# Retention attention with four experts on one Trainium2 core: k^T v as whole-array products early in each tile, a regrouped start of tile 1, and mixing-weight transposes ahead of the first expert product

## The chip, the cores and the metric

The kernel runs on one core of a Trainium2 chip. The metric is device microseconds (us) of one execution. The kernel before took 561.68 us, the median of four runs (560.77, 561.09, 562.26 and 562.52 us). The profiled execution is the one of 560.77 us; the span of its recorded work is 558.9 us.

## The reference, cut to what matters

First comes a causal attention with a decay per head and no softmax, for 8 batches of 8 heads, 576 positions and 64 channels; then four experts whose outputs are mixed by weights that come with each token.

```python
scores = scale * np.matmul(q, k.transpose(0, 1, 3, 2))
Dmat = np.where(rel >= 0, gamma[:, None, None] ** rel[None, :, :], 0.0)
ret = np.matmul(scores * Dmat, v)             # (8, 8, 576, 64)
x = ret.transpose(0, 2, 1, 3).reshape(4608, 512)
p = domain_probs / (domain_probs.sum(-1, keepdims=True) + 1e-09)
for e in range(4):
    h = np.maximum(x @ w1[e], 0.0)            # 512 -> 1024
    out += p[:, e:e + 1] * (h @ w2[e])        # 1024 -> 512
```

## The kernel before, in words

**Experts.** The 4608 tokens are cut into nine tiles of 512. `moe(nt)` is a generator that issues one tile, and each `yield` ends a group. Of each expert it issues eight groups "up" (`up`, L514: four 128x512 matmuls that accumulate over the 512 channels into a PSUM tile `ph`, then ScalarE's Relu into `hT`, L533) and four groups "down" (L543: eight 128x512 matmuls into `po`, then the weighted sum into `acc`: on ScalarE for expert 0, L547, on VectorE for the others, L549). So a tile has 48 groups: groups 0 to 7 are up and 8 to 11 down of expert 0, 12 to 19 up of expert 1, 24 to 31 up of expert 2, 36 to 43 up and 44 to 47 down of expert 3. `ph` and `po` share three PSUM banks (`ps_mm`).

With `lead=3`, as tiles 0 and 1 have it, the first three up groups are split by columns: first the left 256 tokens of all three, then, group by group, the right 256. The extra yields let other work stand in between.

**Attention.** A tile needs `xT`, the attention's output transposed. Tile nt reads tokens of batches nt-1 and nt (a batch is 576 tokens), so the attention of later batches is issued between the expert groups. `plan` holds, for each tile, what is called after which group; the order on every engine is the order of issue. Four chunks of 128 positions and a remainder of 64 make a batch. GpSimd casts k, q and v to bf16 (`km`, `qm`, `vm`, remainder `krb`, `qrb`, `vrb`; L235 to L243); k carries its decay. The transposes `qkT` come from TensorE in batches 0 and 1 (`T`, `Tc`, `Trem`) and from SyncE's transposing DMAs in batches 2 to 7 (`dmaT`, L268, issued by `begin` after the casts; then follow the loads of the next batch, on the same queue). Scores: `S`, `Sc`, `Srem`, masked on VectorE into `sT`. Outputs: products of masked scores with v (`O_values`, L351, and L358 for the remainder), then products of q with the running sum of k^T v over earlier chunks (`O_states`, L365, and L371), and a VectorE product with the decay `gq` into `xT`.

**k^T v.** The running sum stands in `sbd`, one 128x128 block for each chunk and pair of heads, of which the two diagonal 64x64 blocks are used. In batches 2 to 7 `kv_all` (L389) runs once per batch after group 24: 32 matmuls with 64 columns of k as weights and 64 columns of v moving, one per chunk and head, even heads into PSUM partitions 0 to 63 and odd heads into 64 to 127. `kv_sum` then adds the four chunks up: ScalarE copies the first, VectorE makes three sums (L406, L408), GpSimd puts them into `sbd` (L403). In batch 1 `kv(c)` (L250) does the same per chunk, accumulating in PSUM (`kvp`, one bank), with two ScalarE copies per chunk (L255). Batch 0 has its own class, `AttP`.

**Batch 1 and the start of tile 1.** `Tc(c)` follows groups 40, 42, 44 and 46 of tile 0; after the next group come `Sc(c)`, `Oc(c-1)` and `kv(c)`. `Sc(3)` comes after group 47. Then two steps of tile 1 are taken by hand (the left halves of its three first up groups), and then `Oc(3)`, whose `xT` the right halves need.

**Start.** Batch 0's loads and casts, the first expert's weights (`load_w1(0, ...)`, L125, `load_w2(0)`, L130, issued by GpSimd), then `late_constants` and the other experts' weights, on GpSimd too. `mixing_weights` transposes the mixing probabilities on TensorE (L206) after group 1 of tile 0 and normalises them on VectorE. The remainder's loads of batch 0 wait until `w2` of expert 0 has landed.

Of the kernel before, what the change touches and what calls it, by code (L numbers as in the profile page):

```python
# [20 lines left out]
def kernel(  # L21
# [84 lines left out]
    def load_rem(b, gate=None):  # L106
        for n, src in SRC:
            if n == "v":
                t = state[b]["vr"] = raw.tile([128, NP, D], FP32, tag="vr", name="raw_vr")
                for j in range(2):  # L110
                    nc.sync.dma_start(out=t[64 * j:64 * j + 64],
                                      in_=src[b, j:H:2, SM:S, :].rearrange("h p d -> p h d"))
                continue
            state[b][n + "r"] = raw.tile([R, H, D], FP32, tag=n + "r", name=f"raw_{n}r")
            i = nc.sync.dma_start(out=state[b][n + "r"], in_=src[b, :, SM:S, :].rearrange("h p d -> p h d"))
            if gate is not None and n == "k":
                after(i, gate)
# [38 lines left out]
    make_identity(nc, ident)  # L156

# [6 lines left out]
    identf = const.tile([NTT, NTT], FP32)  # L164


    trir = const.tile([128, R], BF16)

    def late_constants():
        nc.gpsimd.memset(tri, 1.0)  # L170
        nc.gpsimd.memset(trir, 1.0)
        for j in (0, 64):
            nc.gpsimd.affine_select(out=trir[j:j + 64], in_=trir[j:j + 64], compare_op=mybir.AluOpType.is_ge,
                                    fill=0.0, base=0, channel_multiplier=-1, pattern=[[1, R]])
        nc.gpsimd.affine_select(out=tri, in_=tri, compare_op=mybir.AluOpType.is_ge, fill=0.0,
                                base=0, channel_multiplier=-1, pattern=[[1, 128]])
        nc.gpsimd.tensor_copy(identf, ident[:NTT, :NTT])
# [25 lines left out]
    def mixing_weights():  # L203
        pp = ps_at.tile([128, E, NTT], FP32, tag="at", name="pp")
        for e in range(E):
            nc.tensor.transpose(pp[:, e, :], probs_raw[:, :, e], identf)  # L206
        nc.vector.tensor_copy(probs, pp)
        nc.vector.tensor_reduce(psm, probs[:, :, :].rearrange("p e t -> p t e"),
                                axis=mybir.AxisListType.X, op=ADD)
        nc.vector.tensor_scalar_add(psm, psm, 1e-9)  # L210
        nc.vector.reciprocal(psm, psm)
        nc.vector.tensor_tensor(probs, probs, psm[:, :].unsqueeze(1).to_broadcast([128, E, NTT]), op=MULT)
# [7 lines left out]
    class Att:  # L220
        rem_states = (NCH - 1,)

        def __init__(self, b):
# [3 lines left out]
            self.r = {n: att1.tile([R, H, D], BF16, tag=n + "r", name=n + "rb") for n in "kq"}  # L227
            self.r["v"] = att1.tile([128, NP, D], BF16, tag="vr", name="vrb")
# [16 lines left out]
        def kv(self, n):  # L245
            if n == 0:
                self.kvp = ps_kv.tile([128, NP, D], FP32, tag="kv", name="kvp")
            for p in range(NP):
                for j in range(2):
                    nc.tensor.matmul(  # L250
                        self.kvp[64 * j:64 * j + 64, p, :], lhsT=self.m["k"][:, n, 2 * p + j, :],
                        rhs=self.m["v"][:, n, 2 * p + j, :],
                        start=(n == 0 and p == 0), stop=(n == NCH - 1), skip_group_check=True)
            for j in (0, 64):
                nc.scalar.activation(sbd[j:j + 64, n, :, j:j + 64], self.kvp[j:j + 64], Copy)  # L255
# [75 lines left out]
        def Srem(self):  # L331
            s = ps_at.tile([128, NP, R], FP32, tag="at", name="sr")
            for p in range(NP):
                for j in (0, 64):
                    r = slice(j, j + 64)
                    nc.tensor.matmul(s[r, p, :], lhsT=self.qkT[r, 1, p, SM:S], rhs=self.qkT[r, 0, p, SM:S],
                                     start=True, stop=True, skip_group_check=True)
            self.srem = s

        def Srem_mask(self):  # L340
            st = self.sT["r"] = att1.tile([128, NP, R], BF16, tag="sTr", name="sTr")
            nc.vector.tensor_tensor(st, self.srem, trir[:, :].unsqueeze(1).to_broadcast([128, NP, R]), op=MULT)


        def O_values(self, pairs, rem=False):
            self.os = [ps_at.tile([128, SM], FP32, tag="at", name="o") for _ in pairs]
            self.orem = ps_at.tile([128, NP, R], FP32, tag="at", name="orem") if rem else None
            for p, o in zip(pairs, self.os):
# [5 lines left out]
            if rem:  # L354
                for p in range(NP):
                    for j in (0, 64):
                        r = slice(j, j + 64)
                        nc.tensor.matmul(self.orem[r, p, :], lhsT=self.r["v"][r, p, :], rhs=self.sT["r"][r, p, :],  # L358
                                         start=(p == 0), stop=False, skip_group_check=True)

        def O_states(self, pairs, rem=False):
            b = self.b
            for p, o in zip(pairs, self.os):
# [4 lines left out]
            if rem:  # L368
                for n in self.rem_states:
                    for p in range(NP):  # L370
                        nc.tensor.matmul(self.orem[:, p, :], lhsT=sbd[:, n, p, :], rhs=self.qkT[:, 0, p, SM:S],  # L371
                                         start=False, stop=(p == NP - 1), skip_group_check=True)
            for p, o in zip(pairs, self.os):
                nc.vector.tensor_tensor(xT[:, p, b * S:b * S + SM], o, gq[:, p, 0:SM], op=MULT)  # L374
            if rem:
                nc.vector.tensor_tensor(xT[:, :, b * S + SM:(b + 1) * S], self.orem, gq[:, :, SM:S], op=MULT)

        def Orem(self):
            self.O_values([], rem=True)
            self.O_states([], rem=True)  # L380


        def kv_all(self):
            self.kvp = [ps_kv.tile([128, 2, NP, D], FP32, tag="kv", name="kva"),
                        ps_at.tile([128, 2, NP, D], FP32, tag="at", name="kvb")]
            for n in range(NCH):
                for p in range(NP):
                    for j in range(2):
                        nc.tensor.matmul(self.kvp[n // 2][64 * j:64 * j + 64, n % 2, p, :],  # L389
                                         lhsT=self.m["k"][:, n, 2 * p + j, :], rhs=self.m["v"][:, n, 2 * p + j, :],  # L390
                                         start=(n % 2 == 0 and p == 0), stop=True, skip_group_check=True)

        def kv_sum(self):
            ksum = att1.tile([128, NCH, NP, D], FP32, tag="ksum", name="ksum")
            parts = [self.kvp[n // 2][:, n % 2] for n in range(NCH)]

            def put(eng, src, n):
                for j in (0, 64):
                    r = slice(j, j + 64)
                    if eng is nc.scalar:  # L400
                        eng.activation(sbd[r, n, :, r], src[r], Copy)  # L401
                    else:
                        eng.tensor_copy(sbd[r, n, :, r], src[r])  # L403

            put(nc.scalar, parts[0], 0)
            nc.vector.tensor_copy(ksum[:, 0], parts[0])  # L406
            for n in range(1, NCH):
                nc.vector.tensor_tensor(ksum[:, n], ksum[:, n - 1], parts[n], op=ADD)  # L408
                put(nc.gpsimd, ksum[:, n], n)
# [99 lines left out]
    def moe(nt, lead=0):  # L509
# [8 lines left out]
        for e in range(E):  # L518
            hT = hpool.tile([128, NFC, NT], BF16, tag="hT")
            for fc in range(NFC):  # L520
                if e == 0 and fc < lead:
                    if fc == 0:
                        early = [ps_mm.tile([128, NT], FP32, tag="mm", name="ph") for _ in range(lead)]
                        for x in range(lead):
                            up(early[x], e, x, slice(0, NT // 2))
                            if x != 1:
                                yield
                    ph = early[fc]
                    up(ph, e, fc, slice(NT // 2, NT))
# [29 lines left out]
    tiles = [moe(nt, lead=3 if nt < 2 else 0) for nt in range(n_nt)]  # L559
# [4 lines left out]
    for x, (hf, u) in enumerate(UNITS):  # L564
# [16 lines left out]
        a0.kv(hf, u)  # L581
    next(tile0)
# [13 lines left out]
    for nt in range(n_nt):  # L596
# [5 lines left out]
        if nt == 0:  # L602
# [3 lines left out]
            at(22, a0.Srem, a0.Srem_mask)  # L606
# [13 lines left out]
            for c, g in enumerate((40, 42, 44, 46)):  # L620
                at(g, lambda c=c: state["a1"].Tc(c))
                if c < 3:
                    at(g + 1, lambda c=c: state["a1"].Sc(c))
                if c > 0:
                    at(g + 1, lambda c=c: state["a1"].Oc(c - 1))
                at(g + 1, lambda c=c: state["a1"].kv(c))
        elif nt + 1 < B:
            if nt == 1:
# [3 lines left out]
                at(4, a1.Srem, a1.Srem_mask)  # L632
                at(6, a1.Orem)
            def begin(b=nt + 1):
# [10 lines left out]
            at(7 if nt == 1 else 0, begin)  # L645
            at(19 if nt == 1 else 17, lambda: state["A"].S([0, 1]))
            at(24, lambda: state["A"].Srem(), lambda: state["A"].O_values([0, 1]),
               lambda: state["A"].kv_all(), lambda: state["A"].kv_sum(), lambda: state["A"].Srem_mask())
            at(28, lambda: state["A"].O_states([0, 1]))
            at(30, lambda: state["A"].S([2, 3]))  # L650
            at(34, lambda: state["A"].O_values([2, 3], rem=True), lambda: state["A"].O_states([2, 3], rem=True))
# [3 lines left out]
        if nt == 0:  # L655
            state["a1"].Sc(3)
            next(tiles[1])
            next(tiles[1])
            state["a1"].Oc(3)
# [30 lines left out]
```

## Time and profile before

| | |
|---|---|
| median of four runs | 561.68 us |
| profiled execution | 560.77 us |
| its span | 558.9 us |
| granted TensorE clock, mean | 1.0 |
| up and down products, 128x512, back to back | 6.91 us for 32 |
| one steady tile (from one tile's first expert-0 down group to the next's: 153.26 to 212.96 us, 212.96 to 272.65 us) | 59.7 us |
| ScalarE Relu of an up group | 597 ns |
| ScalarE copy of one chunk's k^T v half, 64x256 | 378 ns |
| VectorE sum of a down group | 751 ns |

TensorE's matmuls are recorded with a modelled end, so they overlap in the records; the distance from one start to the next start is what a matmul takes of the stream. A line of the timeline gives a group's start, the time it covers, engine, line, operation, tiles and count, and in brackets what the engine waited for. A few records are missing, so that a group can count 15 matmuls where 16 ran.

### The profile page before, as it was taken

The page shows a single profiled execution, that of the slowest core. Times are in us where ns is not written, and L with a number is a line of the kernel's source. Part 1 is how long each engine was busy: PE and PEld are TensorE (multiplying, and loading weights), DVE is VectorE, ACT ScalarE, POOL GpSimd, SP SyncE. Part 2 cuts the span into 40 slices and gives each one's busy share as a digit, 9 for nine tenths or more (in the row PEclk, how much of TensorE's full clock was granted, in tenths as well). Part 3 has the DMA queues.
Part 4 walks back from the last instruction along what each step waited for, and adds up shares of the span by engine and source line. Part 5 has one row for each costly group of instructions (what it writes and reads, how often), then busy time and mean ns, then how long its engine had stood idle before and what let it go on. Part 6 is the DMA issues. An engine that isn't in the chain of part 4 may idle for free.

```text
span 558.9 us, 8453 instructions
## 1 busy us (share of the span) xinstructions
PE 546.2 (98%) x3469; PEld 262.8 (47%) x3530; DVE 165.7 (30%) x283; ACT 216.9 (39%) x371; POOL 109.5 (20%) x182
## 2 busy tenths in 40 slices
PE   8899999999999999999999999999999999999997
PEld 4544454454445444454445444544444444444443
DVE  5402261253214520462035212542046202220222
ACT  6452344433353235223433334323532353335332
POOL 7611257026002520044002600260010000000000
PEclk9999999999999999999999999999999999999999
DMA  8999999491369025910594058703300100010001
GB/s 233 180 202 200 206 204 234 102 210 20 106 132 178 1 86 96 215 21 38 114 182 83 0 123 149 143 1 96 65 2 1 74 2 0 1 75 1 1 0 75
DMA packets 148277, 53.83 MB, mean 96 GB/s; under 512 B 130668, under 2 KB 142188, under 8 KB 148240
## 3 DMA queue, kind: packets, MB, share of 16 engines
q1 hardware_dynamic: 141296, 44.79, 39.0%
q0 software_dynamic: 6800, 8.39, 8.8%
q8 instruction: 27, 0.44, 0.4%
q10 hardware_dynamic: 144, 0.13, 0.1%
q14 instruction: 10, 0.08, 0.1%
HBM read 45.16 MB, written 9.44 MB: 98 GB/s over the span
## 4 chain that ended last, share of the span: by engine, by line
PE 90%; DMA 5%; SPq 3%; POOL 1%; issue 1%; DVE 0%; POOLq 0%
PE po L543 43%; PE ph L514 41%; DMA wt<-in_moe_w_dram 2%; SPq L268 1%; PE o L351 1%; PE s L276 1%; DMA raw_v<-in_v_dram 1%; DMA raw_k<-in_k_dram 1%; PE o L365 1%; SPq L85 1%; SPq L91 1%; DMA qkT<-km 0%; POOL km L423 0%; PE ptc L297 0%; PE orem L358 0%
## 5 line engine op out<-in xcount | busy, mean ns | idle before, releaser
L533 ACT ACTIVATE hT<-ph 128x512 bf16<-128x512 f32 x288 | 171.6, 597 | 275.1 <-PE ph L514 275.1
L514 PE MATMUL ph<-xT,wt 128*128 128x512 bf16 (+1 forms) x1149 | 258.3, 375 | 2.4 <-DVE xT L329 0.8
L543 PE MATMUL po<-wt,hT 128*128 128x512 bf16 (+1 forms) x1126 | 254.0, 378 | 3.1 <-DMA wt<-in_moe_w_dram 1.3
L543 PEld LDWEIGHTS <-hT 128*128 128x128 bf16 x1160 | 112.6, 98 | 134.1 <-DMA wt<-in_moe_w_dram 1.8
L514 PEld LDWEIGHTS <-wt 128*128 128x128 bf16 x1176 | 112.7, 98 | 129.1 <-issue 0.9
L549 DVE SCALAR_TENSOR_TENSOR acc<-po,probs,acc 128x512 f32<-128x512 f32 (+1 forms) x109 | 81.3, 746 | 234.2 <-PE po L543 226.3
L283 DVE TENSOR_TENSOR sT<-s,tri 128x512 bf16<-128x512 f32 x48 | 29.8, 684 | 113.4 <-PE s L276 113.4
L403 POOL CAST sbd<-ksum 64x256 bf16<-64x256 f32 x36 | 14.3, 396 | 221.8 <-DVE ksum L408 197.7
L547 ACT ACTIVATE acc<-po,probs 128x512 f32<-128x512 f32 x36 | 24.7, 687 | 39.7 <-PE po L543 38.7
L235 POOL TENSOR_TENSOR km<-raw_k,gk 128x512 bf16<-128x512 f32 x28 | 29.2, 1042 | 14.2 <-DMA raw_k<-in_k_dram 10.2
L237 POOL CAST vm<-raw_v 128x512 bf16<-128x512 f32 x28 | 17.2, 614 | 42.3 <-PE o L351 35.0
L237 POOL CAST qm<-raw_q 128x512 bf16<-128x512 f32 x28 | 17.1, 609 | 7.6 <-DMA raw_q<-in_q_dram 7.1
L374 DVE TENSOR_TENSOR xT<-o,gq 128x512 bf16<-128x512 f32 x24 | 15.5, 686 | 7.6 <-PE o L365 7.6
L240 POOL TENSOR_TENSOR krb<-raw_kr,gk 64x512 bf16<-64x512 f32 x8 | 8.3, 1036 | 13.1 <-DMA raw_kr<-in_k_dram 12.8
L276 PEld LDWEIGHTS <-qkT 64*128 64x128 bf16 x192 | 5.4, 94 | 5.5 <-issue 4.7
L276 PE MATMUL s<-qkT 64*128 64x128 bf16 x192 | 7.6, 217 | 0.2 <-DMA qkT<-km 0.2
L351 PE MATMUL o<-sT,vm 128*64 128x128 bf16 x192 | 7.6, 222 | 0.0
L351 PEld LDWEIGHTS <-vm 128*64 128x64 bf16 x192 | 5.7, 109 | 2.8 <-issue 2.5
L140 PE MATMUL warm_out<-warm_in 128*128 128x512 bf16 x14 | 5.2, 524 | 1.3 <-DVE warm_in L135 1.3
L406 DVE COPY ksum<-kva 128x256 f32<-128x256 f32 x6 | 2.5, 425 | 11.8 <-ACT sbd L401 11.8
L365 PE MATMUL o<-qkT,sbd 128*128 128x128 bf16 x72 | 6.0, 220 | 0.0
L313 DVE TENSOR_TENSOR sT<-s,tri 128x512 bf16<-128x512 f32 x8 | 5.1, 684 | 2.0 <-PE s L309 2.0
(94 smaller groups left out, 146.3 us busy)
## 6 DMA issues: line engine op xcount, KB each, us to landing
out_dram<-acc SPq DMA_DIRECT2D x35, 256.0 KB, 2.0
raw_k<-in_k_dram SPq DMA_DIRECT2D x32, 256.0 KB, 5.0
raw_q<-in_q_dram SPq DMA_DIRECT2D x32, 256.0 KB, 5.2
raw_v<-in_v_dram SPq DMA_DIRECT2D x32, 256.0 KB, 5.1
wt<-in_moe_w_dram POOLq DMA_DIRECT2D x7, 1024.0 KB, 24.8
wt<-in_moe_w_dram POOLq DMA_DIRECT2D x2, 512.0 KB, 5.6
raw_kr<-in_k_dram SPq DMA_DIRECT2D x8, 128.0 KB, 5.4
raw_qr<-in_q_dram SPq DMA_DIRECT2D x8, 128.0 KB, 5.0
```

Source lines behind the costliest of these rows:

```text
L235: eng.tensor_tensor(o, i, gk[:, c, :].unsqueeze(2).to_broadcast([128, H, D]), op=MULT)
L237: eng.tensor_copy(o, i)
L276: nc.tensor.matmul(s[j][:, c, :], lhsT=self.qkT[r, 1, p, cs], rhs=self.qkT[r, 0, p, cs], start=True, stop=True)
L283: nc.vector.tensor_tensor(st[:, j], s[j], tri[:, :].unsqueeze(1).to_broadcast([128, NCH, C]), op=MULT)
L351: nc.tensor.matmul(o[64 * j:64 * j + 64, c * C:(c + 1) * C], lhsT=self.m["v"][:, c, 2 * p + j, :], rhs=self.sT[p][:, j, c, :], start=(c == ...
L374: nc.vector.tensor_tensor(xT[:, p, b * S:b * S + SM], o, gq[:, p, 0:SM], op=MULT)
L403: eng.tensor_copy(sbd[r, n, :, r], src[r])
L514: nc.tensor.matmul(ph[:, ts], lhsT=w1_sb[e][:, dc, fc * 128:(fc + 1) * 128], rhs=xT[:, dc, n0 + ts.start:n0 + ts.stop], start=(dc == 0), s ...
L533: nc.scalar.activation(hT[:, fc, :], ph, Relu)
L543: nc.tensor.matmul(po, lhsT=hT[:, fc, ns * 128:(ns + 1) * 128], rhs=w2_sb[e][:, fc, d:d + w], start=(fc == 0), stop=(fc == NFC - 1))
L547: nc.scalar.activation(a, po, Copy, scale=pe)
L549: nc.vector.scalar_tensor_tensor(a, po, pe, a, op0=MULT, op1=ADD)
```

## The change

- `kv(n, pairs)` is now one matmul per chunk and pair of heads, 128 columns of k as weights and 128 of v moving; only the diagonal blocks of the result are copied. It accumulates over the chunks in one PSUM bank, and two ScalarE copies per chunk put the running sum into `sbd`. `kv_all` and `kv_sum` are gone.
- In batches 2 to 7 the four `kv` follow groups 9, 11, 13 and 15 of a tile (13, 15, 17 and 18 of tile 1). `O_values` and `O_states` are one function again, `O`, issued after groups 24 and 32; the second `S` follows group 27, not 30.
- The remainder's v has the layout of k and q: one load instead of two (`load_rem`); `Srem` writes two PSUM tiles and is masked by two VectorE products with a corner of `tri`; `trir` is gone.
- Batch 1: `Tc` follows groups 39, 41, 43 and 45, and `kv(c)`, `Sc(c)`, `Oc(c-1)` follow the group after; `Oc(3)` follows group 47. Nothing of tile 1 is issued ahead of it.
- Tile 1 splits its first two up groups at column 384 (left 384 of both, then right 128 of each), not its first three at column 256.
- The transposes of the mixing probabilities are issued before the first up group of tile 0 and use a bank of `ps_mm`; `identf`, which they need, is made at the kernel's start instead of in `late_constants`.

```diff
-            for p in range(NP):
-                for j in range(2):
-                    nc.tensor.matmul(
-                        self.kvp[64 * j:64 * j + 64, p, :], lhsT=self.m["k"][:, n, 2 * p + j, :],
-                        rhs=self.m["v"][:, n, 2 * p + j, :],
-                        start=(n == 0 and p == 0), stop=(n == NCH - 1), skip_group_check=True)
+            for i, p in enumerate(pairs):
+                h = slice(2 * p, 2 * p + 2)
+                nc.tensor.matmul(
+                    self.kvp[:, p, :], lhsT=flat(self.m["k"][:, n, h, :]), rhs=flat(self.m["v"][:, n, h, :]),
+                    start=(n == 0 and i == 0), stop=(n == NCH - 1), skip_group_check=True)
+            a, z = pairs[0], pairs[-1] + 1
             for j in (0, 64):
-                nc.scalar.activation(sbd[j:j + 64, n, :, j:j + 64], self.kvp[j:j + 64], Copy)
+                nc.scalar.activation(sbd[j:j + 64, n, a:z, j:j + 64],
+                                     self.kvp[j:j + 64, a:z, j:j + 64], Copy)
...
-    tiles = [moe(nt, lead=3 if nt < 2 else 0) for nt in range(n_nt)]
+    tiles = [moe(0, lead=3, pause=True), moe(1, lead=2, cut=3 * NT // 4)] + [moe(nt) for nt in range(2, n_nt)]
...
         a0.kv(hf, u)
+    transposed_probs()
     next(tile0)
...
-            for c, g in enumerate((40, 42, 44, 46)):
+            for c, g in enumerate((39, 41, 43, 45)):
                 at(g, lambda c=c: state["a1"].Tc(c))
-                if c < 3:
-                    at(g + 1, lambda c=c: state["a1"].Sc(c))
+                at(g + 1, lambda c=c: state["a1"].kv(c, allp), lambda c=c: state["a1"].Sc(c))
                 if c > 0:
                     at(g + 1, lambda c=c: state["a1"].Oc(c - 1))
-                at(g + 1, lambda c=c: state["a1"].kv(c))
+            at(47, lambda: state["a1"].Oc(3))
...
+            for n, g in zip(range(NCH), (13, 15, 17, 18) if nt == 1 else (9, 11, 13, 15)):
+                at(g, lambda n=n: state["A"].kv(n, allp))
             at(19 if nt == 1 else 17, lambda: state["A"].S([0, 1]))
-            at(24, lambda: state["A"].Srem(), lambda: state["A"].O_values([0, 1]),
-               lambda: state["A"].kv_all(), lambda: state["A"].kv_sum(), lambda: state["A"].Srem_mask())
-            at(28, lambda: state["A"].O_states([0, 1]))
-            at(30, lambda: state["A"].S([2, 3]))
-            at(34, lambda: state["A"].O_values([2, 3], rem=True), lambda: state["A"].O_states([2, 3], rem=True))
+            at(24, lambda: state["A"].Srem(), lambda: state["A"].O([0, 1]))
+            at(27, lambda: state["A"].S([2, 3]))
+            at(32, lambda: state["A"].O([2, 3], rem=True))
...
-            state["a1"].Sc(3)
-            next(tiles[1])
-            next(tiles[1])
-            state["a1"].Oc(3)
```

## The prediction

> **What bounds the kernel.** I read the page's shares and the chain that ended last, then the list of waits, then TensorE's timeline at the places that the change touches.
>
> ```profile
> PE 546.2 (98%) x3469; PEld 262.8 (47%) x3530; DVE 165.7 (30%) x283; ACT 216.9 (39%) x371; POOL 109.5 (20%) x182
> ...
> PE 90%; DMA 5%; SPq 3%; POOL 1%; issue 1%; DVE 0%; POOLq 0%
> ```
>
> TensorE is 98% busy and makes 90% of the chain; no other engine is above 39%. So a change counts by what it adds to TensorE's stream or takes out of it, or by a wait there. The list of waits has three on the way:
>
> ```profile
> PE po L543 <- DMA wt<-in_moe_w_dram: 1.3, 1, 1.3
> ...
> PE ph L514 <- DVE xT L329: 0.8, 1, 0.8
> ...
> PE s L276 <- DMA qkT<-km: 0.2, 1, 0.2
> ```
>
> The first is the first down group waiting for expert 0's `w2`, at 27.4 us; the second the right halves of tile 1's first up groups waiting for batch 1's last `xT`; the third batch 2's scores waiting for its last transposing DMA. Together 2.3 us: more than that no rearrangement of waits can bring.
>
> Then TensorE's stream around group 24 of tile 1, which is the same in tiles 2 to 6:
>
> ```profile
> 114.78 1.03 PE L514 MATMUL ph<-xT,wt 128*128 128x512 bf16 x4
> 115.74 0.31 PE L336 MATMUL sr<-qkT 64*64 64x64 bf16 x8
> 115.98 0.64 PE L351 MATMUL o<-sT,vm 128*64 128x128 bf16 x16
> 116.45 0.42 PE L389 MATMUL kva<-vm,km 128*64 128x64 bf16 x16
> 116.70 0.42 PE L389 MATMUL kvb<-vm,km 128*64 128x64 bf16 x16
> 117.06 3.63 PE L514 MATMUL ph<-xT,wt 128*128 128x512 bf16 x15
> 120.52 0.50 PE L365 MATMUL o<-qkT,sbd 128*128 128x128 bf16 x6
> 120.86 1.89 PE L514 MATMUL ph<-xT,wt 128*128 128x512 bf16 x8
> ```
>
> Only starts matter. A 128x512 matmul takes 6.91/32 = 0.216 us, an up group 0.864, a down group 1.73. The four at 114.78 end at 115.64, but the next, on quarter arrays, start at 115.74: going from whole array to parts costs 0.10 us. The 32 `kv_all` matmuls run from 116.45 to 117.06; 0.10 of that is the way back to the whole array (the 16 `s` from 122.68 to 123.23, 0.55 us, carry the same), so they take 0.51, 16 ns each: the two column halves run side by side. The six `o` at L365, whole array and 128 columns, take 120.86 - 120.52 = 0.34, 56 ns each, and no pause before or after: 117.06 + 16 x 0.216 = 120.52.
>
> **The change, part by part.**
>
> *k^T v in batches 2 to 7.* Removed: 0.51 us per batch. Added: 16 whole-array matmuls of 128 columns, which the trace has at L365: 16 x 56 ns = 0.90, in four places without a change of array form. `O` keeps its three changes of form. So +0.39 us per batch, +2.34 for six: all on the path, since TensorE is the bound. The eight transposes of a `Tc`, whole array and 128 columns too, give 0.45/8 = 56 again. What these rows do not show is a pause ahead of the first of four, which waits for GpSimd and ScalarE: at least 0, at most the 0.10 of a change of form, 24 x 0.10 = 2.4 in all. I take 0, since the first `o` at L365 also waits for another engine's `sbd` and follows without a pause. The Trainium skill, "TensorE: Matmul & The Clock Gate", section "Back-to-back issue gap", speaks harder against the change: it gives about 81 ns per 128-column matmul in a stream of weight loads and matmuls. An estimate from that figure is 6 x (16 x 0.081 - 0.51) = 4.7 us for the six batches instead of 2.3. L365 is such a stream at 56, so the row decides.
>
> What goes with `kv_sum`, three VectorE sums and six GpSimd casts per batch, was off the path (VectorE 30%, GpSimd 20%): nothing gained. GpSimd's casts for the next batch may start after group 15 instead of 24; SyncE's transposes and loads stay behind the tile's output stores, so no transfer moves in tiles 2 to 6. ScalarE gets 8 copies instead of 2 per batch, 6 x 378 ns = 2.3 us in a tile of 59.7 with ScalarE 39% busy; in up groups it idles 0.27 us of each 0.864. It matters through one wait: the chunks accumulate in one PSUM bank, so `kv(n+1)` waits until ScalarE has copied `kv(n)`, and those copies queue behind a Relu. The rows:
>
> ```profile
> 116.91 0.77 ACT L401 ACTIVATE sbd<-kva 64x256 bf16<-64x256 f32 x2 [0.41 <-PE kva L389]
> 118.13 0.60 ACT L533 ACTIVATE hT<-ph 128x512 bf16<-128x512 f32 x1 [0.45 <-PE ph L514]
> 118.99 0.60 ACT L533 ACTIVATE hT<-ph 128x512 bf16<-128x512 f32 x1 [0.27 <-PE ph L514]
> ```
>
> A pair of copies is 0.77, a Relu 0.60, and it starts 0.2 after its group. Stepped through tile 1 from the end of group 13 (0.224 for `kv` and 0.864 per group, so groups 14 to 18 end at 1.09, 1.95, 3.04, 3.90 and 4.99): copies of chunk 0 until 1.45 us, of chunk 1 until 3.40, Relus of 16 and 17 until 4.69, copies of chunk 2 from 4.58 (engine times overlap by 0.1) to 5.35. But chunk 3 is due after group 18, at 4.99. TensorE stands 0.43 us, and group 19 and the scores stand behind it. In tiles 2 to 6 the last two are two groups apart (13, 15): copies end at 3.40 after group 11, TensorE wants 3.90; 0.5 spare, no wait. Also no `ph` bank is late: Relus stay within two groups.
>
> *Batch 1 and tile 1's start.*
>
> ```profile
> 82.84 0.40 PE L309 MATMUL s<-qkT 64*128 64x128 bf16 x8
> 83.17 1.48 PE L514 MATMUL ph<-xT,wt 128*128 128x256 bf16 x12
> 84.58 0.44 PE L322 MATMUL oc<-sT,vm 128*64 128x128 bf16 x8
> 84.95 0.40 PE L327 MATMUL oc<-qkT,sbd 128*128 128x128 bf16 x4
> 86.13 1.47 PE L514 MATMUL ph<-xT,wt 128*128 128x256 bf16 x12 [0.78 <-DVE xT L329]
> 87.53 0.29 PE L261 MATMUL ptr<-ident,qrb 64*128 64x64 bf16 x4
> ```
>
> I rebuilt the stretch from the first `Tc` (67.60 us, now 66.73, a group sooner) to `Trem` at 87.53. Blocks, as the starts of before give them: four `Tc` at 0.447; four `kv` at 0.224; four `Sc` at 0.095 + 0.327; the `Oc` 0.346, 0.57, 0.57 and, alone, 0.665; four up 3.454 and four down 6.908; tile 1's two split groups 8 x 0.162 + 8 x 0.056 (384 and 128 columns at the rate of 512) and a whole one, 2.61; 0.095 to `Trem`. Sum 19.59, so `Trem` starts at 86.32: 1.21 us sooner. Of that 0.78 is the wait, the rest changes of form (`kv` had to go back to column halves after the whole-array part of `Oc`). The wait goes because the left 384 columns (1.30 us) now stand behind `Oc(3)` and cover the 0.96 us that `xT` needed (84.95 + 0.22 to 86.13); VectorE's sum of group 47 (0.75) comes first, which leaves 0.2 us to spare. If that cover fails, up to 0.78 returns. Casts are in time: `vm` of chunk 1 ends at 69.6 us, its `kv` now at 70.9; `qm` of chunk 2 at 71.75, its `Tc` at 72.7.
>
> *What is late next.* Batch 2's scores after group 19 of tile 1. TensorE reaches them at 106.92 before; now -1.21 + 0.90 (four `kv`) + 0.43 (the stall) = 107.04. Their last transposing DMA lands at 107.44. That chain starts at GpSimd's `vrb`, and eight transposes of 1.25 us on SyncE's queue follow. It moves a little: one remainder load less on SyncE ahead of it in batches 1 and 2 (0.6 us of issue each), but the new `vrb` cast is 0.60 instead of 0.39. I bound it by 0 and -0.6, so the scores end between 0.28 us sooner and as before; taken: 0.14 sooner. So most of the 1.21 is spent here. Then tile 1 drops its `kv_all`, 0.51.
>
> *Start.* The probability transposes leave the stream at 20.53 (0.59 us) and stand before the first up group, where TensorE idles 0.2. But all of this is before 27.37, where TensorE waits 1.32 us for `w2`: worth nothing, and the wait grows. `w2`'s issue on GpSimd (16.01) does not move; `identf` (0.21) fits into the 0.55 us that GpSimd waits for the first k. Behind `w2`, 0.90 us of constants go (`trir` 0.17 + 0.52, `identf` 0.21), so the next weights are issued that much sooner; at worst they share with `w2` and it lands 0.45 later, at best nothing: I take 0. `Srem` and `Orem` keep eight matmuls each in pairs; VectorE's second mask (0.42) is done 1.3 us before its reader.
>
> **Sum** against the profiled 560.77: -0.14 (to the end of batch 2's scores) - 0.51 + 5 x 0.39 (tiles 2 to 6) = +1.3, which gives 562.1. The profiled execution is the fastest of four; the same step on their median of 561.68 gives **563.0**.
>
> **Rivals.**
> - *The wait returns* (chance 0.12): VectorE gets to `xT` behind its group-47 sum too late, or group 18's stall is larger; nothing is gained up to the scores and 0.6 is lost. +1.9 to +2.1: 563.7, just slower than 0.3%. For it: only 0.2 us spare. Against: 1.30 covers 0.96.
> - *ScalarE becomes the pace of k^T v* (0.24): if its queue is 0.5 us later than stepped, chunk 3 waits in each tile, as in tile 1. Place: group 15 of tiles 2 to 6. Price 0.43 x 5 = 2.15: 565.2, slower. It decides once copies end over 0.5 us later, for instance if copies and Relus never overlap. Against: the spare 0.5 us, and a ScalarE that is 39% busy.
> - *The lead is kept* (0.04 for faster): without the stall, and with batch 2's transposes out of the way, the scores start at 106.92 - 1.21 + 0.90 = 106.61 and end at 107.16 instead of 107.87: -0.71 - 0.51 + 1.95 = +0.7. Only if `w2` also landed earlier by its whole 1.32 us would it be -0.6 (561.1), and past 0.3% it takes something that no row shows. `w2`'s issue waits for batch 0's casts, which don't move.
> - *The forecast* (0.60): within 0.3%.
>
> **Numbers.** A measurement tells about 0.3%, 1.7 us, from no change. Low end: +0.7 if batch 2's transposes hold nothing up and there is no stall, less 1.0, by which the fastest run shown lies below the median: 561.4. High end: the second rival, 565.2. Faster 0.04, same 0.60, slower 0.12 + 0.24 = 0.36.
>
> **What would show it.** `kv` (L238) four in 0.22 us with ups right behind; steady tiles of 59.7 + 0.39 = 60.1; no wait on `xT` at tile 1's start, `Trem` at 86.3; a wait of TensorE for ScalarE of about 0.4 us after group 18 of tile 1 alone; the `w2` wait at about 1.5. Wrong if steady tiles are over 60.3 or below 59.8.

## The result, and the profile after

| | before | after |
|---|---|---|
| median, measured side by side | 561.33 us (55 runs) | 562.44 us (34 runs) |
| ratio, 95% interval | | 1.0021 [1.0016, 1.0026] |
| profiled execution, its span | 560.77, 558.9 us | 562.87, 561.1 us |
| first down group starts (first w2 has landed) | 27.37 us | 28.21 us |
| from there to `Trem` of tile 1 | 60.17 us | 59.01 us |
| from there to batch 2's scores, first to last start | 79.55 to 80.35 us | 79.80 to 80.21 us |
| one steady tile | 59.69 us | 60.08 us |
| from the first down group to the last matmul | 527.71 us | 529.01 us |

The change costs 1.2 us, with an interval of 0.9 to 1.5. The prediction had 1.3 on top of the median of before.

The two profiled executions did not start alike. In that of after the third of batch 0's loads of k landed later (6.63 us in the chain instead of 5.87), so `w2` was issued at 16.71 instead of 16.01 us and the first down group began 0.85 us later. That differs between executions of one kernel too, as the repeated runs below show, so all stretches here are counted from the first down group.

The page of after, its shares and its chain:

```profile
PE 549.4 (98%) x3353; PEld 265.9 (47%) x3414; DVE 158.7 (28%) x267; ACT 227.3 (41%) x407; POOL 96.8 (17%) x143
...
PE 93%; DMA 3%; POOL 1%; issue 1%; SPq 1%; ACT 0%; DVE 0%; ACTq 0%
```

TensorE has fewer instructions (3353, not 3469) and is busy longer. ScalarE took over copies (41%, not 39%), VectorE and GpSimd lost work; neither shows in the time. Everything stands or falls with TensorE's stream. Its list of waits:

```profile
PE po L499 <- DMA wt<-in_moe_w_dram: 0.4, 1, 0.4
PE kvp L238 <- ACT sbd L243: 0.4, 1, 0.4
```

The wait on `xT` (0.8) and the one on batch 2's transposing DMA (0.2) are gone; a wait of k^T v for ScalarE's copies has come, once. The `w2` wait reads 0.4 because TensorE itself came late to it in this execution: it waited 1.6 us for a cast and ran at about half rate for a while (last section).

TensorE around the end of tile 0 and the start of tile 1:

```profile
82.12 1.89 PE L499 MATMUL po<-wt,hT 128*128 128x512 bf16 x8
83.94 0.41 PE L311 MATMUL oc<-sT,vm 128*64 128x128 bf16 x8
84.29 0.40 PE L316 MATMUL oc<-qkT,sbd 128*128 128x128 bf16 x4
84.52 2.77 PE L470 MATMUL ph<-xT,wt 128*128 128x384 bf16 x19
87.22 0.29 PE L250 MATMUL ptr<-ident,qrb 64*128 64x64 bf16 x4
```

The 384 columns follow `Oc(3)` at once. The right 128 columns, which need its `xT`, come inside the same line without a wait: eight left matmuls of 0.162 us bring TensorE to them at 85.82, which is where the first one starts. (The line counts 19 of 20 matmuls; one record is missing.) VectorE had written that `xT` by 85.41:

```profile
84.72 0.69 DVE L318 TENSOR_TENSOR xT<-oc,gq 128x512 bf16<-128x512 f32 x1
```

TensorE around group 18 of tile 1:

```profile
103.28 0.39 PE L238 MATMUL kvp<-vm,km 128*128 128x128 bf16 x4
103.51 1.89 PE L470 MATMUL ph<-xT,wt 128*128 128x512 bf16 x8
105.23 0.39 PE L238 MATMUL kvp<-vm,km 128*128 128x128 bf16 x4
105.46 1.03 PE L470 MATMUL ph<-xT,wt 128*128 128x512 bf16 x4
106.84 0.38 PE L238 MATMUL kvp<-vm,km 128*128 128x128 bf16 x4 [0.36 <-ACT sbd L243]
107.06 1.03 PE L470 MATMUL ph<-xT,wt 128*128 128x512 bf16 x4
108.02 0.62 PE L265 MATMUL s<-qkT 64*128 64x128 bf16 x16
```

Read starts only. Four `kv` take 0.23 (105.23 to 105.46) and the next up group follows at once. Group 18 starts at 105.46 and its four matmuls take 0.86, so chunk 3 was due at 106.32; it starts at 106.84, 0.52 late. (The bracket has 0.36 because the modelled ends of the matmuls reach into the gap.) ScalarE in that stretch:

```profile
105.93 0.77 ACT L243 ACTIVATE sbd<-kvp 64x256 bf16<-64x256 f32 x2
106.72 0.60 ACT L489 ACTIVATE hT<-ph 128x512 bf16<-128x512 f32 x1
107.32 0.78 ACT L243 ACTIVATE sbd<-kvp 64x256 bf16<-64x256 f32 x2
```

Chunk 2's two copies end at 106.70, and TensorE goes on 0.14 later. And the steady tiles, in the chain in order of time (start, length, work), where the same stretch returns once per tile:

```profile
168.66 7.07 PE po L499 x32
...
228.75 7.07 PE po L499 x32
...
288.83 7.07 PE po L499 x32
```

60.09 and 60.08 us apart, where the tiles of before were 59.7 apart. Group 24 of tile 1, to be laid beside the rows of before:

```profile
115.49 1.03 PE L470 MATMUL ph<-xT,wt 128*128 128x512 bf16 x4
116.44 0.31 PE L325 MATMUL sr<-qkT 64*64 64x64 bf16 x8
116.69 0.64 PE L340 MATMUL o<-sT,vm 128*64 128x128 bf16 x16
117.26 0.51 PE L351 MATMUL o<-qkT,sbd 128*128 128x128 bf16 x6
117.60 2.75 PE L470 MATMUL ph<-xT,wt 128*128 128x512 bf16 x11
```

The two `kva`, `kvb` rows are missing between `o` and what follows; the changes of array form around the `o` stay.

### The profile page after: what moved, and what is told of

Same layout as the page of the kernel before. It is cut to its first block, busy times and chain, and to the rows that moved or that the text cites. A ratio compares the mean times of both kernels' runs of the same rounds, so it can differ in the third digit from the quotient of the medians.

```text
span 561.1 us, 8230 instructions
## 1 busy us (share of the span) xinstructions
PE 549.4 (98%) x3353; PEld 265.9 (47%) x3414; DVE 158.7 (28%) x267; ACT 227.3 (41%) x407; POOL 96.8 (17%) x143
## 4 chain that ended last, share of the span: by engine, by line
PE 93%; DMA 3%; POOL 1%; issue 1%; SPq 1%; ACT 0%; DVE 0%; ACTq 0%
PE po L499 44%; PE ph L470 43%; DMA wt<-in_moe_w_dram 2%; PE o L340 1%; PE s L265 1%; DMA raw_k<-in_k_dram 1%; PE kvp L238 1%; PE o L351 1%; SPq L85 1%; POOL km L379 0%; PE sr L325 0%; PE orem L346 0%; PE ptc L286 0%; POOL wt L119 0%; PE oc L311 0%
## 5 line engine op out<-in xcount | busy, mean ns | idle before, releaser
L470 PE MATMUL ph<-xT,wt 128*128 128x512 bf16 (+2 forms) x1140 | 258.4, 375 | 1.6 <-issue 0.2
L272 DVE TENSOR_TENSOR sT<-s,tri 128x512 bf16<-128x512 f32 x48 | 29.8, 684 | 124.1 <-PE s L265 124.1
L243 ACT ACTIVATE sbd<-kvp 64x256 bf16<-64x256 f32 x56 | 20.8, 372 | 3.0 <-PE kvp L238 2.7
L238 PEld LDWEIGHTS <-km 128*128 128x128 bf16 x112 | 8.5, 98 | 7.2 <-issue 0.8
L238 PE MATMUL kvp<-vm,km 128*128 128x128 bf16 x112 | 10.8, 219 | 0.4 <-ACT sbd L243 0.4
L329 DVE TENSOR_TENSOR sTr<-sr,tri 64x256 bf16<-64x256 f32 x16 | 6.0, 411 | 3.4 <-PE sr L325 3.4
```

What stands on the lines that cost most here:

```text
L238: nc.tensor.matmul(self.kvp[:, p, :], lhsT=flat(self.m["k"][:, n, h, :]), rhs=flat(self.m["v"][:, n, h, :]), start=(n == 0 and i == 0), st ...
L243: nc.scalar.activation(sbd[j:j + 64, n, a:z, j:j + 64], self.kvp[j:j + 64, a:z, j:j + 64], Copy)
L272: nc.vector.tensor_tensor(st[:, j], s[j], tri[:, :].unsqueeze(1).to_broadcast([128, NCH, C]), op=MULT)
L470: nc.tensor.matmul(ph[:, ts], lhsT=w1_sb[e][:, dc, fc * 128:(fc + 1) * 128], rhs=xT[:, dc, n0 + ts.start:n0 + ts.stop], start=(dc == 0), s ...
```

## The experiments

Each ratio goes by runs of before on the same chip (medians 561.27 us beside e1 to e4, 561.22 beside e5 to e7). "Stream" is the time from the first down group to the last matmul in the profile, against 527.71 of the profiled before.

| run | what | median, us | ratio, 95% | stream | steady tile |
|---|---|---|---|---|---|
| after | the whole change | 562.44 | 1.0021 [1.0016, 1.0026] | +1.30 | 60.08 |
| e1_start_only | batch 1 and tile 1's start alone | 560.23 | 0.999 [0.9977, 1.0002] | -1.15 | 59.69 |
| e2_kv_only | k^T v of batches 2 to 7 alone | 563.55 | 1.004 [1.0028, 1.0052] | +2.46 | 60.08 |
| e3_late_scores | e1, batch 2's scores a group later | 559.14 | 0.9961 [0.9949, 0.9973] | -1.56 | 59.69 |
| e4_no_stall | after, tile 1's `kv` a group or two earlier | 561.94 | 1.001 [1.0001, 1.0019] | +0.79 | 60.08 |
| e5_kv_halves | after, `kv` on column halves | 565.17 | 1.0069 [1.0056, 1.0081] | +4.23 | 60.59 |
| e6_mixing_only | the mixing transposes alone | 561.41 | 1.0003 [0.9994, 1.0012] | +0.69 | 59.69 |
| e7_late_scores_w2 | e3, first w2 in two halves | 559.59 | 0.9973 [0.9963, 0.9984] | +0.37 | 59.69 |
| e8_before_again | before, profiled once more | 561.27 (one run) | | +0.56 | 59.69 |

The last row is the measure for the "stream" column: two profiles of the same kernel differ by 0.56 us, so a smaller difference there counts only if a line of the trace carries it.

**The start alone, e1.** On the kernel before:

```diff
-            for c, g in enumerate((40, 42, 44, 46)):
+            for c, g in enumerate((39, 41, 43, 45)):
                 at(g, lambda c=c: state["a1"].Tc(c))
...
+                at(g + 1, lambda c=c: state["a1"].kvw(c), lambda c=c: state["a1"].Sc(c))
...
+            at(47, lambda: state["a1"].Oc(3))
...
+    tiles = [moe(0, lead=3, pause=True), moe(1, lead=2, cut=3 * NT // 4)] + [moe(nt) for nt in range(2, n_nt)]
```

`kvw` is the whole-array `kv` of after; `kv_all` stays in batches 2 to 7.

> The kernel before with the new start of tile 1 alone (batch 1's units a group sooner, its k^T v as whole-array products, Oc(3) after group 47, tile 1 led by two three-quarter groups); batches 2 to 7 keep their one block of column halves. Theory (the lead is spent waiting): Trem about 1.2 us sooner, then TensorE stands 1.2 to 1.5 us before the last chunk of batch 2's scores in tile 1, whose transposing DMA lands as late as before; time 0 to -0.3 us against before, ratio 0.9995 to 1.000. Rival (the lead is kept, each part adds up by itself): no such wait over 0.3 us, -1.2 us, ratio 0.998.

Measured: a median 1.04 us below that of before; the ratio's interval goes from 1.3 us faster to 0.1 slower. In the profile `Trem` stands at 59.01 after the first down group, 1.16 sooner, and the scores at 78.39 to 79.20, also 1.16 and 1.15 sooner. They did wait for the transposing DMA, but no longer than before:

```profile
106.15 0.34 PE L287 MATMUL s<-qkT 64*128 64x128 bf16 x6
106.72 0.45 PE L287 MATMUL s<-qkT 64*128 64x128 bf16 x10 [0.23 <-DMA qkT<-km]
107.11 3.19 PE L554 MATMUL po<-wt,hT 128*128 128x512 bf16 x14
```

The bracket was 0.22 in the profile of before. So the theory that the lead is spent here fell in this execution: the first transposing DMA was issued 67.12 us after the first down group, not 68.36. Why is taken up under e8.

**k^T v alone, e2.** The kernel before with the four `kv` after groups 9, 11, 13, 15 (13, 15, 17, 18 in tile 1) in place of `kv_all` and `kv_sum`:

```diff
+            for n, g in zip(range(NCH), (13, 15, 17, 18) if nt == 1 else (9, 11, 13, 15)):
+                at(g, lambda n=n: state["A"].kvw(n))
             at(19 if nt == 1 else 17, lambda: state["A"].S([0, 1]))
-            at(24, lambda: state["A"].Srem(), lambda: state["A"].O_values([0, 1]),
-               lambda: state["A"].kv_all(), lambda: state["A"].kv_sum(), lambda: state["A"].Srem_mask())
+            at(24, lambda: state["A"].Srem(), lambda: state["A"].O_values([0, 1]),
+               lambda: state["A"].Srem_mask())
```

> The kernel before with whole-array k^T v in four places per tile for batches 2 to 7 alone; start of tile 1 as before. Theory: +0.90 for the four and +0.5 for the wait after group 18 ahead of batch 2's scores, of which the wait for the transposing DMA (0.22) goes; -0.51 for the block that is gone; 5 x 0.39 in tiles 2 to 6: +3.1 to +3.2 at most, +2.5 if the scores' wait covers more; ratio 1.0045 to 1.0057, steady tiles of 60.08 us. Rival 1 (parts add up): after minus the start's 1.2, that is +2.3 to +2.4, the same size, so this run tells only together with the first one: theory wants the two parts to sum to more than the whole change (about +2.8 against +1.1), the rival to the same. Rival 2 (81 ns per product as the skill's page has it): +4.7 or more.

Measured: 1.6 to 2.9 us slower by the ratio, +2.46 in the stream. The terms: six batches of +0.39 are 2.34, and the stall after group 18 is there as in after, 0.52; 0.39 is won back because batch 2's scores no longer wait (16 of them take 0.41 us from first to last start here, 0.80 with the wait in before). That makes 2.47. The streams of e1 and e2 add up: -1.15 + 2.46 = +1.31, against +1.30 for the whole. The medians say the same: -1.04 + 2.28 = +1.24, against +1.1. Since e2 leaves `O` and the remainder's layout as before and its tile takes 60.08 too, those parts of the change cost nothing there. So the whole change is a gain of over one us at the start that is more than paid away by k^T v.

**The stall taken out, e4.** On after:

```diff
-            for n, g in zip(range(NCH), (13, 15, 17, 18) if nt == 1 else (9, 11, 13, 15)):
+            for n, g in zip(range(NCH), (11, 13, 15, 17) if nt == 1 else (9, 11, 13, 15)):
```

> The changed kernel with the k^T v of tile 1 after groups 11, 13, 15 and 17 instead of 13, 15, 17 and 18, so that two groups lie between the third and the fourth. Theory: the 0.52 us wait for ScalarE after group 18 is gone, but a wait of the same size comes at batch 2's scores, whose last transposing DMA lands when the stall let TensorE arrive: 0 to -0.1 us against the changed kernel, ratio to before 1.0018 to 1.0022. Rival (the stall is on the path): -0.5 us, ratio 1.0011 to 1.0013.

Measured: 561.94, against 562.44 for after: 0.50 sooner by the medians, with intervals of the ratios that still touch. The lines:

```profile
103.42 0.39 PE L238 MATMUL kvp<-vm,km 128*128 128x128 bf16 x4
103.64 1.89 PE L470 MATMUL ph<-xT,wt 128*128 128x512 bf16 x8
105.36 0.39 PE L238 MATMUL kvp<-vm,km 128*128 128x128 bf16 x4
105.59 1.89 PE L470 MATMUL ph<-xT,wt 128*128 128x512 bf16 x8
107.41 0.62 PE L265 MATMUL s<-qkT 64*128 64x128 bf16 x16
```

No bracket at the last `kv`, and the scores start 79.29 us after the first down group instead of 79.80: 0.51 sooner, the size of the stall. The rival was right: the stall was on the path, and no wait for the transposes took its place. In this execution the transposes were also early, though (the first at 65.72), so it doesn't show what a late chain would do.

**Batch 2's scores a group later, e3.** On e1:

```diff
-            at(19 if nt == 1 else 17, lambda: state["A"].S([0, 1]))
+            at(20 if nt == 1 else 17, lambda: state["A"].S([0, 1]))
```

> As e1_start_only, but batch 2's first scores in tile 1 follow group 20 instead of 19, one down group (1.73 us) later. Theory: the transposing DMA has landed by then, nothing waits, and the lead of 1.2 us and the 0.22 us wait are kept: -1.2 to -1.5 us, ratio 0.9975 to 0.998. Rival (the lead was never on the path of the end, something after the scores is late too): 0 to -0.3 us.

Measured: 559.14 us, ratio 0.9961 [0.9949, 0.9973], faster than both kernels. A down group (1.73) now stands between group 19 and the scores:

```profile
105.67 1.89 PE L554 MATMUL po<-wt,hT 128*128 128x512 bf16 x8
107.49 0.62 PE L287 MATMUL s<-qkT 64*128 64x128 bf16 x16
108.04 3.19 PE L554 MATMUL po<-wt,hT 128*128 128x512 bf16 x13
```

All 16 scores in a row, no wait. The stream is 1.56 shorter than in before: 1.16 from the start and 0.39 from the wait that is gone. The medians are 2.1 us apart, more than the theory's 1.2 to 1.5; nothing here shows where the other 0.6 comes from.

**Column halves in the new places, e5.** On after, in batches 1 to 7:

```diff
-                nc.tensor.matmul(
-                    self.kvp[:, p, :], lhsT=flat(self.m["k"][:, n, h, :]), rhs=flat(self.m["v"][:, n, h, :]),
-                    start=(n == 0 and i == 0), stop=(n == NCH - 1), skip_group_check=True)
+                for j in range(2):
+                    nc.tensor.matmul(
+                        self.kvp[64 * j:64 * j + 64, p, :], lhsT=self.m["k"][:, n, 2 * p + j, :],
+                        rhs=self.m["v"][:, n, 2 * p + j, :],
+                        start=(n == 0 and p == 0), stop=(n == NCH - 1), skip_group_check=True)
```

> The changed kernel with k^T v by head on column halves, eight matmuls per chunk instead of four, in the same places. Theory (what made the old block cheap was that it stood in one place beside other part-array work): eight take 0.13 to 0.16 us instead of 0.22, but each place now leaves the whole array and comes back, 0.10 us each way, so 0.33 to 0.35 us per place in batches 2 to 7: +0.11 to +0.13 x 24 = +2.6 to +3.1 us against the changed kernel, ratio to before about 1.007. Rival (halves are cheaper wherever they stand): 0.16 - 0.22 per place, -1.5 to -2.4 us against the changed kernel, ratio to before 0.998 to 0.999.

Measured: 565.17 us, ratio 1.0069 [1.0056, 1.0081]; the steady tile takes 60.59, 0.51 more than with whole-array products. The places, in a steady tile:

```profile
161.74 0.32 PE L238 MATMUL kvp<-vm,km 128*64 128x64 bf16 x8
161.98 1.90 PE L469 MATMUL ph<-xT,wt 128*128 128x512 bf16 x8
163.81 0.32 PE L238 MATMUL kvp<-vm,km 128*64 128x64 bf16 x8
164.06 1.90 PE L469 MATMUL ph<-xT,wt 128*128 128x512 bf16 x8
```

Eight up matmuls take 8 x 0.216 = 1.73, but the next halves start 1.83 after them (161.98 to 163.81): 0.10 to go to column halves. The eight and the way back take 0.25. Together 0.35 per place, against 0.224 for the four whole-array products: 4 x 0.125 = 0.50 per tile, as measured. In `kv_all`, between other part-array work, eight halves had cost 0.51/4 = 0.13. The theory held: the halves of before were cheap by where they stood. The Trainium skill, "TensorEngine Tiling (Array Packing)", section "When to Use Tiling", lists a width of weights of 64 or less as the case for column tiling, and "Key Properties" says that changing the mode drains TensorE. This run puts the two on one scale: the first, read alone, speaks for halves here; the drain, 0.10 us on the way in by these starts, decides against them.

**The mixing transposes alone, e6.** On before:

```diff
+    identf = const.tile([NTT, NTT], FP32)
+    nc.gpsimd.tensor_copy(identf, ident[:NTT, :NTT])
...
-    def mixing_weights():
-        pp = ps_at.tile([128, E, NTT], FP32, tag="at", name="pp")
+    def transposed_probs():
+        pp = ps_mm.tile([128, E, NTT], FP32, tag="mm", name="pp")
...
         a0.kv(hf, u)
+    transposed_probs()
     next(tile0)
```

> The kernel before with the probability transposes alone moved ahead of the first up group, and identf made at the start. Theory (hidden by the wait for w2): the first up groups end 0.2 to 0.6 us sooner and TensorE waits that much longer before the first down group; time 0.0 +- 0.3 us, ratio 0.9995 to 1.0005. Rival (0.59 us of the stream is saved): -0.6 us, ratio 0.999.

Measured: 1.0003 [0.9994, 1.0012], no difference that can be told. Its waits:

```profile
PE po L545 <- DMA wt<-in_moe_w_dram: 1.0, 1, 1.0
PE s L278 <- DMA qkT<-km: 0.9, 1, 0.9
```

TensorE still waits 1.0 us for `w2`, so what the stream does before is covered. The 0.69 of its stream is the wait of batch 2's scores, 0.9 in the list here and 0.2 in the profile of before, as in e8; starts give the same, 1.49 us from the first score to the last, not 0.80.

**The first w2 in two halves, e7.** On e3:

```diff
-        return nc.gpsimd.dma_start(out=wt2, in_=moe_w2[e].rearrange("(fc p) d -> p fc d", p=128))
+        src = moe_w2[e].rearrange("(fc p) d -> p fc d", p=128)
+        for fcs in ((slice(0, NFC // 2), slice(NFC // 2, NFC)) if e == 0 else (slice(0, NFC),)):
+            i = nc.gpsimd.dma_start(out=wt2[:, fcs], in_=src[:, fcs])
+        return i
```

> As e3_late_scores, and w2 of the first expert is loaded in two halves of four row blocks each, so that the first down group can begin with the half that is there. Theory (the start waits for the end of w2's transfer, not for its beginning): four products, 0.86 us, run in the old wait of 1.3 us: -0.5 to -0.9 us more than e3, together -2.1 to -2.5 us of stream against before, ratio about 0.995 to 0.996. Rival (a second issue on GpSimd of 0.9 us delays the second half and the other weights by as much): no gain over e3, ratio 0.9965 to 0.9975.

Measured: 559.59 us, 0.9973 [0.9963, 0.9984]; e3 had 559.14. Not better, perhaps a little worse.

```profile
26.50 1.03 PE L557 MATMUL po<-wt,hT 128*128 128x512 bf16 x4
28.45 3.83 PE L557 MATMUL po<-wt,hT 128*128 128x512 bf16 x17 [0.92 <-DMA wt<-in_moe_w_dram]
```

Four products start at 26.50, earlier than in any other profile, and then TensorE waits for the second half until 28.45. In e3, with one load, the same product started at 27.37 + 0.86 = 28.23. So the early start was given back with the second half's late landing: there is no gain, as the rival had it, though why that half landed late was not tried by itself. This row's stream is counted from the earlier start, so it can't be compared with the others. By the span's clock its last matmul starts 1.06 us later than in e3. The second half makes 0.22 of that; 0.85 is lost at batch 2's scores, which wait here although they stand a group later:

```profile
107.69 0.34 PE L290 MATMUL s<-qkT 64*128 64x128 bf16 x6
108.71 0.45 PE L290 MATMUL s<-qkT 64*128 64x128 bf16 x10 [0.68 <-DMA qkT<-km]
```

Sixteen scores take 1.26 us from first to last start, 0.41 in e3. This execution was the longest of the seven of e7.

**The kernel before again, e8.**

> The kernel before once more, for a second profile: is the start of batch 2's transposing DMAs, 68.4 us after the first down product, its own or that execution's? If its own: again 68 to 69 us, one of the four output stores ahead of it takes over 1.2 us to issue, and batch 2's scores wait about 0.2 us. If chance: 67 us, as in e1, and no store over 0.6 us.

Measured: the same steady tile and the same 60.17 to `Trem`, but batch 2's scores wait 0.8 us where they waited 0.2, and end 0.56 later. The transposes are issued by SyncE behind a long row of loads and the four stores of tile 0's output. From the load of k that opens the last batch of loads to the first of those stores it took 17.11 us in before, 17.19 in e8, 17.13 in e1 and 17.11 in e3. What differs is mostly the stores (in e1 and e3 that load of k also came 0.35 and 0.46 us sooner than in before). SyncE's queue (start, length, line, operation) in the profile of before:

```profile
92.15 2.96 SPq L552 DMA_DIRECT2D out_dram<-acc  x4
95.73 1.32 SPq L268 DMA_TRANSPOSE qkT<-qm  x1
```

The same in the profile of after:

```profile
92.32 2.20 SPq L508 DMA_DIRECT2D out_dram<-acc  x4
94.72 1.54 SPq L257 DMA_TRANSPOSE qkT<-qm  x1
96.31 2.21 SPq L257 DMA_TRANSPOSE qkT<-km  x1
```

In before, e2, e5, e6, e7 and e8 one of the four stores took 1.34 to 1.78 us to issue; in after, e1, e3 and e4 all four took 0.37 to 0.57. The first transpose follows accordingly: 68.1 to 70.4 us after the first down group in the six (the 70.4 is e7's, counted from its earlier start), 65.7 to 67.1 in the four. In after this lead was lost again, since the second transpose took 2.21 us to issue: the last one was issued until 78.71 us after the first down group, 78.83 in before. Since e5 and e7 have the new start and a long store, the start alone doesn't decide it. What does was not found, and stays open; for one execution it is worth up to about one us at the scores. A group of slack covered it in e3; in e7, with a long store, it did not.

## Why the prediction was right, step by step

- **k^T v, +0.39 per steady tile.** 60.08 against 59.69, as worked out, and e2 gives it alone. The row at L365, 56 ns per 128-column matmul, was the right one, and no pause came ahead of the four. The Trainium skill's 81 ns ("TensorE: Matmul & The Clock Gate", "Back-to-back issue gap") would have made it 0.79; the traces don't bear it out here.
- **ScalarE's copies in tiles 2 to 6.** No wait there: the list has a single wait of k^T v for `sbd`, in tile 1. The rival at 565.2 did not come about.
- **Tile 1's start, 1.21 sooner.** 1.16. The missing 0.05 is no wait: it comes in steps of about 0.01, mostly where TensorE goes back to whole-array products. The cover held, with 0.41 us between the end of `xT` (85.41) and the start of the right columns (85.82), where 0.2 had been reckoned.
- **The stall after group 18, 0.43.** 0.52. The copies of chunk 2 ended at 106.70, which is 5.37 after the start of chunk 0's `kv` where the stepping had 5.35; the rest is the 0.14 from there to TensorE's start, which the stepping had set at about half. e4 confirmed that it is paid.
- **Scores 0.14 sooner.** They are (80.21 against 80.35), but partly for another reason than given. The sum had them held by the transposes. In fact -1.16 + 0.90 + 0.52 brings TensorE there 0.26 later than before at the first score, and no score waits. The last transposing DMA was issued until 106.93, and the trace has it landed at 108.12; the seventh score, the first that waited in before, starts at 108.20. Both bounds met there within a tenth of a us in this execution. Since the transposes move by more than that from one execution to the next (e8), it is in part luck that the 0.14 came out.
- **Where that chain starts.** The prediction said at GpSimd's `vrb`. That is wrong: in e1 the first transpose was issued 67.12 us after the first down group, before the `vrb` cast began (67.82), and in e5 2.0 us before it. SyncE's own queue holds it: in all ten profiles it follows the last of the four stores by 0.20 to 0.62 us.
- **"Most of the 1.21 is spent here."** Wrong as a mechanism. e1 keeps all of it at the scores and e3 in the time. In after the four `kv` of tile 1 and the stall (0.90 + 0.52) take it up ahead of the scores, not a wait for the transposes.
- **The mixing transposes, worth nothing.** e6: 1.0003 [0.9994, 1.0012]. That the `w2` wait grows to about 1.5 was not seen: it was 0.4 in after and 1.0 in e6, since arrival and landing both vary from one execution to the next.
- **The sum, +1.3.** -0.14 - 0.51 + 5 x 0.39 = +1.30, and +1.30 in the profile from the first down group on. The medians differ by 1.1, the interval of the ratio gives 0.9 to 1.5. (For the low end of its range the prediction put the fastest run 1.0 below the median; it lies 0.91 below.)

## What to carry to other kernels

The price of a small matmul goes with its neighbours: eight column halves cost 0.13 us between other part-array work and 0.35 alone between whole-array groups, while four whole-array products cost 0.22 in every place they were put. When a stage is led forward, look at the next gate on the way and give it slack in the same edit: here moving the scores one group further back (e3) turned a gain that could hardly be measured into 0.4%, of which the streams explain 1.56 us, 0.3%. A chain that accumulates in one PSUM bank and is copied out each time ties TensorE to the queue of the copying engine; step through that queue wherever two links stand one group apart.

## What was not expected of the hardware

- In the profiles of after and e2 the granted clock was 0.54 and 0.57 from 12.4 to 19.3 us; in the other eight it was 1.0 there. Just these two had a long wait of TensorE shortly before, 1.60 us until 9.88 and 1.27 until 10.04; the others had none over 0.8 in that place. The length of the wait alone doesn't decide it: in e4 TensorE waited 2.27 us for `w2`, and the granted clock was 1.0 before, during and after.

```profile
28.12 4.06 PE L499 MATMUL po<-wt,hT 128*128 128x512 bf16 x18 [2.27 <-DMA wt<-in_moe_w_dram]
```

  What lowers it wasn't tried by itself and stays open. Three stretches of after (stretch, length, busy time of PE, PEld, DVE, ACT and POOL with counts, granted clock, share and rate of the DMA engines):

```profile
10.00:12.40 2.40, 2.15 (x50) 1.40 (x49) 1.86 (x5) 1.62 (x4) 2.15 (x4) 0.89 1.03 273
12.40:19.30 6.90, 6.90 (x104) 5.06 (x104) 4.79 (x10) 2.62 (x8) 6.82 (x11) 0.54 1.02 175
19.30:24.00 4.70, 4.65 (x55) 3.73 (x55) 2.97 (x9) 2.08 (x5) 3.76 (x5) 1.00 1.03 152
```

  The second row has 0.54 where its neighbours have 0.89 and 1.00. It lay before the wait for `w2`, which covered it: TensorE still waited 0.4 us there.
- A mean granted clock under 0.999 is on record for seven of the runs of after (0.994 to 0.997), with the four longest, 564.10 to 564.57 us, among them; the others have a median of 562.4, so the result doesn't hang on these. One or two runs each of e1, e2, e4 and e6 show it too, and none of the 40 of before that were measured beside the experiments. Why the kernels differ in this isn't shown.
- The start of the first down group differed from execution to execution, 26.84 to 28.46 us in the nine profiles with one `w2` load, though the kernels begin nearly alike: 1.6 us, more than the whole effect under study.
- SyncE's issue of one 256 KB store took 0.33 to 0.57 us. The long ones, 1.34 to 1.78, all stand among tile 0's first four, right behind the loads: one in six of the ten profiles.
